# Conversion of the float64 weights written out slot by slot over block 0's FFN, in an attention and FFN kernel on one Trainium2 core

## The chip, the cores and the metric

The kernel runs on one core of a Trainium2 chip. The metric is device microseconds (us) from the start to the end of one execution; several executions are timed and the median counts. Lower is better. Engines are named as in the profile: PE (TensorE, matmul; PEld is its weight load), DVE (VectorE), ACT (ScalarE), POOL (GpSimd), SP (SyncE, which here issues most DMAs).

## The reference

Two stages. The first is an attention-like recurrence with a 48x48 state for each of 4 sequences and 8 heads, over 768 positions; the second a two-layer FFN on the 3072 rows of 384 values that the first one leaves.

```
k_n = k / (norm(k) + 1e-6)
for t in range(768):
    y[t]  = q[t] @ state
    v_old = state @ k_n[t]            # over the key axis
    state = state + beta[t] * outer(k_n[t], v[t] - v_old)
x = y as [3072, 384]
h = x @ w_in                          # [384, 2048]
out = max(0.01 * h, h) @ w_out        # [2048, 384]
```

The two weight matrices come as float64; the kernel computes in float32, and converts the weights on the chip, by bit operations on the raw 8-byte words.

## The kernel before

**Blocks.** The 768 positions are cut into 12 blocks of 64; one block of the 4 sequences is 256 token rows. The recurrence inside a block is replaced by a triangular system of 64 steps for each of the 32 sequence-head pairs. A block n needs, in this order: `gram(n)` (products of k with k and with q on PE, tiles pg, pq, and their masking by DVE into rq), `inv` (the norms in `norms`, then 31 elimination steps on DVE in `eliminate`, lines L390 and L395, on a tile T; blocks 0 and 1 are inverted together as T0, block 2 as T1, block 3 as T2 and so on), `solve(n)` (merging the inverted halves, tiles pz and pu; then pk, pw, py, pc on PE, each copied out of PSUM by ACT into rt, rv, ys), `columns(n)` (transposes px, and the split of x into xh on ACT, L123, and xl on DVE, L124) and `ffn(n)`. From block 2 on the inverse goes through DRAM: T to the DRAM tiles td and tt, and from these to the squares sq, which the matmuls pz and pu of `merge_z` and `merge_u` read (L490).

**FFN.** `ffn(n)` runs over 16 chunks f of the 2048 hidden columns: matmuls ph (L725), the leaky relu on ACT into gh (L728), and matmuls po (L715), which run two chunks behind. Block 0 uses plain float32 weights w32, views of the tiles cg: 3 matmuls of ph and 2 of po for each chunk. Every later block uses the format fp32r in two parts (high and low, tile w): 9 matmuls of ph and 6 of po for each chunk, a second relu on ACT, and gl by a subtraction on DVE (L733).

**Weights.** Eight pieces j of two chunks each. A raw piece wr is loaded by SP. Then, all in the generator `weights()`: the top 16 bits of each word are packed as bfloat16 into cg (on ACT, L155, for j of 0 to 3; on DVE, L158, for 4 to 7); four DVE operations with bits (L159, L162, L163, L165) build sign, exponent and first mantissa bits, the last of them into a tile ch of its own; ACT spreads ch over cg (L167); and `finish()` ors in the other mantissa bits on DVE (L176). After that cg holds the float32 piece, which block 0's FFN reads. `lows()` later makes the two parts for the blocks that follow: ACT rounds cg into the high part (L188), DVE subtracts for the low part (L190). There are NG = 4 buffers for cg, so `weights()` calls `lows()` for piece j-4 before it starts piece j; the parts w4 to w7 are made at the end of block 0 and at the start of block 1. The tile w of a piece takes the place of its raw words wr.

**What sets the order.** Each engine runs its instructions in program order. `weave` calls the generators in turn, slot by slot (a slot is about one chunk f of the FFN); the tuples SV, IV and GG give the slots between which `solve`, `inv` and `gram` of the next blocks are spread. Before block 0's FFN the calls are written out one by one. A scheduler then orders within those bounds; `behind(name)` keeps an instruction behind the last one recorded in `mark[name]` on its engine.

Of the kernel before, what the change touches and what calls it, by code (L numbers as in the profile page):

```python
# [26 lines left out]
NGR = NSEQ // GS  # L27
# [20 lines left out]
def delta_moe_kernel(ctx: ExitStack, tc, kq0, kqT, kv, qT, beta, cst, w_all, out, nblk):  # L48
# [89 lines left out]
    later, w32 = [], {}

    def weights():  # L140

        left = []
        for j in range(NJ):
            if j >= NG:
                next(lw)
            raw = raws.pop(j)
            mid = raw.bitcast(U32).rearrange("p (n two) -> p two n", two=2)[:, 0]
            top = raw.bitcast(BF16).rearrange("p (n four) -> p four n", four=4)[:, 2]  # L150
            g = sb.tile([P, 4 * DO], F32, tag=f"c{j % NG}", name=f"cg{j}", bufs=1)
            gi = g.bitcast(U32)
            a, x = gi[:, 0:2 * DO], gi[:, 2 * DO:]
            if j in BYA:
# [13 lines left out]
            left.append((j, g, mid))  # L168
            while left[1 if KA <= j < NJ - 1 or not j else 0:]:
                finish(*left.pop(0))  # L170
            yield

    def finish(j, g, mid):
        gi = g.bitcast(U32)
        with behind("work"):
            i = nc.vector.scalar_tensor_tensor(gi, mid, 13, gi, ALU.logical_shift_right, ALU.bitwise_or)  # L176
        mark["conv"] = mark["gl"] = i.ins
        later.append((j, g))
        for e in range(2):
            w32[2 * j + e] = g[:, e * 2 * DO:(e + 1) * 2 * DO]  # L180

    def lows():
        while True:
            j, g = later.pop(0)
            t = sb.tile([P, 8 * DO], F32R, tag=f"w{j}", name=f"w{j}", bufs=1)
            hi, lo = t[:, 0:4 * DO], t[:, 4 * DO:]
            with behind("xh"):
                nc.scalar.copy(hi, g)  # L188
            with behind("conv"):
                nc.vector.tensor_tensor(lo, g, hi.bitcast(F32), ALU.subtract)  # L190
            for y, part in enumerate((hi, lo)):
                for e in range(2):
                    for x, w in enumerate((wi, wo)):
                        w[y][2 * j + e] = part[:, (2 * e + x) * DO:(2 * e + x + 1) * DO]
            yield
# [10 lines left out]
    def first():  # L206
# [69 lines left out]

# [405 lines left out]
    def columns(n):  # L682

        need(sv, solve, n)
        xs[n] = parts = []
        px = [ps_a.tile([P, 2, TB], F32, tag="a", name=f"px{n}_{i}") for i in range(2)]
        part = [px[cc // 2][:, cc % 2] for cc in range(NCC)]
        for cc, x in enumerate(part):
            for g in range(NGR):
                i = nc.tensor.transpose(x[:, g * P:(g + 1) * P], ys[n, g][:, cc * P:(cc + 1) * P], eye)  # L690
        mark["px"] = i.ins
        for cc, x in enumerate(part):
            if not n:
                parts.append(sb.tile([P, TB], F32, tag="xh", name=f"x0_{cc}", bufs=3))
                if not cc % 2:
                    mark["xh"] = nc.scalar.copy(parts[-1], x).ins
                else:
                    mark["x"] = nc.vector.tensor_copy(parts[-1], x).ins
                continue
            xh, xl = (sb.tile([P, TB], F32R, tag=t, name=f"{t}{n}_{cc}", bufs=3) for t in ("xh", "xl"))  # L700
            split(x, xh, xl)
            parts.append((xh, xl))

    def ffn(n):
# [15 lines left out]
        for f in range(NFC):  # L720
            ph = hbank[f % 2][:, f // 2 % 2]
            ways = [(wi[y][f], x[cc][e], cc) for cc in range(NCC) for y, e in ((0, 0), (0, 1), (1, 0))] if n else [
                (w32[f], x[cc], cc) for cc in range(NCC)]
            for k, (w, a, cc) in enumerate(ways):
                i = nc.tensor.matmul(ph, w[:, cc * P:(cc + 1) * P], a, start=(k == 0), stop=(k + 1 == len(ways)))  # L725
            mark["ph"] = i.ins
            gh = sb.tile([P, TB], F32R if n else F32, tag="gh", name=f"gh{n}_{f}", bufs=FB)
            i = nc.scalar.activation(gh, ph, AF.Prelu, alpha=0.01)  # L728
            gl = None
            if n:  # L730
                gl = sb.tile([P, TB], F32R, tag="gl", name=f"gl{n}_{f}", bufs=FB)
# [36 lines left out]
    def weave(n_slots, *streams):

        taken = [0] * len(streams)  # L770
        for i in range(n_slots):
            for k, (gen, steps, a, b) in enumerate(streams):
                want = steps if i >= b - 1 else min(steps, max(0, i + 1 - a) * steps // (b - a))
                while taken[k] < want:
                    next(gen, None)
                    taken[k] += 1
# [107 lines left out]
```

## Time and profile before

| | before |
|---|---|
| median of 3 runs | 643.58 us (642.8 to 644.76) |
| the profiled execution | 642.36 us |
| its span, first to last instruction | 640.5 us |
| PE busy | 587.3 us, 92% of the span |
| DVE busy | 437.5 us, 68% |
| ACT busy | 324.0 us, 51% |
| mean granted TensorE clock | 0.979 |

All times inside an execution are counted from the span's start. The profiled execution lies 1.2 us under the median and takes 1.9 us more than its span. Busy shares are means over the whole span: the first 60 us, in which the first inverse and the first solve run, and the blocks 0 to 2 behind them look different from the blocks after them. A wait names the engine and line that ended it; an engine can also stand still because an instruction ahead of it in its own queue waits.

### The profile page before, as it was taken

To read this page: it belongs to the slowest core of one execution; us is meant where nothing else is said; L and a number is where in the kernel's file an instruction comes from. 1 tells how busy PE (TensorE), PEld (TensorE's weight loads), DVE (VectorE), ACT (ScalarE), POOL (GpSimd) and SP (SyncE) were. 2 spreads that over 40 slices of the span, in tenths; PEclk is the share of its full clock that TensorE was granted. 3 is DMA by queue.
4 is the path that set the end of the run, shared out by engine and by line. 5 is a ranking of instruction groups with operands and counts; after the bars stand their busy time and mean duration, and the time that the engine had idled before them with its cause. 6 is when DMAs were issued, how large, how long until landed. Compare 5 with 4: busy or idle time off the path is not lost.

```text
span 640.5 us, 22374 instructions
## 1 busy us (share of the span) xinstructions
PE 587.3 (92%) x9122; PEld 537.7 (84%) x9122; DVE 437.5 (68%) x1953; ACT 324.0 (51%) x812; POOL 10.7 (2%) x17
## 2 busy tenths in 40 slices
PE   5266987999889999999999999999999999999996
PEld 4245775799677988999999999999999999999996
DVE  3997796998936967859759759759759669331211
ACT  3466845464445544645645536545545545545322
POOL 6000000000000000000000000000000000000000
PEclk9986997999989999999999999999999999999999
DMA  6983754051257362254353352462461540410101
GB/s 122 316 241 125 248 154 111 12 124 27 36 101 157 79 130 55 61 97 104 72 97 95 76 114 71 90 126 47 96 139 27 104 105 4 79 30 3 26 2 26
DMA packets 123431, 59.69 MB, mean 93 GB/s; under 512 B 111296, under 2 KB 114496, under 8 KB 122304
## 3 DMA queue, kind: packets, MB, share of 16 engines
q1 hardware_dynamic: 120576, 57.27, 39.4%
q10 hardware_dynamic: 2752, 0.98, 0.8%
q8 instruction: 72, 1.18, 0.8%
q14 instruction: 31, 0.25, 0.1%
HBM read 46.96 MB, written 11.27 MB: 91 GB/s over the span
## 4 chain that ended last, share of the span: by engine, by line
PE 73%; ACT 3%; DMA 3%; SPq 2%; issue 2%; DVE 1%; ACTq 0%; DVEq 0%
PE ph L725 30%; PE po L715 28%; PE pk L620 3%; PE py L657 3%; PE pw L637 2%; PE pc L647 2%; PE pg L309 2%; DMA tt<-T 1%; PE px L690 1%; PE pu L490 1%; ACT w L188 1%; ACT gh L728 1%; PE pz L490 1%; DMA sq<-tt 1%; DMA td<-T 1%
## 5 line engine op out<-in xcount | busy, mean ns | idle before, releaser
L725 PE MATMUL ph<-xh,w 128*128 128x256 f32 x1056 | 224.5, 289 | 1.7 <-ACT xh L123 1.4
L725 PEld LDWEIGHTS ph<-xh,w 128*128 128x128 f32 x1056 | 174.9, 189 | 8.9 <-ACT xh L123 1.8
L733 DVE TENSOR_TENSOR gl<-ph,gh 128x256 fp32r<-128x256 f32 x176 | 74.3, 423 | 148.3 <-ACT ph L732 146.0
L715 PE MATMUL po<-w,gh 128*128 128x384 f32 x704 | 171.4, 342 | 4.1 <-ACT gh L728 4.1
L728 ACT ACTIVATE gh<-ph 128x256 fp32r<-128x256 f32 (+1 forms) x192 | 73.6, 384 | 170.3 <-PE ph L725 160.5
L725 PE MATMUL ph<-xl,w 128*128 128x256 f32 x528 | 149.3, 284 | 0.0
L715 PEld LDWEIGHTS po<-w,gh 128*128 128x128 f32 x704 | 121.4, 188 | 8.3 <-ACT gh L728 6.7
L395 DVE TENSOR_TENSOR T<-T,tmp 128x60 f32<-128x60 f32 (+35 forms) x661 | 112.3, 207 | 0.8
L390 DVE TENSOR_TENSOR tmp<-T,L 128x60 f32<-128x60 f32 (+35 forms) x661 | 112.2, 208 | 0.9
L715 PE MATMUL po<-w,gl 128*128 128x384 f32 x352 | 105.1, 338 | 0.0
L725 PEld LDWEIGHTS ph<-xl,w 128*128 128x128 f32 x528 | 100.1, 190 | 1.3 <-DVE xl L124 0.3
L732 ACT ACTIVATE ph<-ph 128x256 f32<-128x256 f32 x176 | 66.9, 380 | 0.0
L715 PEld LDWEIGHTS po<-w,gl 128*128 128x128 f32 x352 | 60.8, 188 | 0.4 <-issue 0.4
L622 ACT ACTIVATE rt<-pk 48x512 f32<-48x512 f32 x44 | 26.1, 594 | 25.1 <-PE pk L620 24.3
L326 DVE TENSOR_TENSOR rq<-pg,csb 64x256 f32<-64x256 f32 x80 | 33.9, 423 | 4.6 <-ACT gs L313 3.2
L725 PE MATMUL ph<-x,cg 128*128 128x256 f32 x96 | 26.6, 423 | 4.3 <-DVE rq L269 4.3
L639 ACT COPY rv<-pw 64x384 f32<-64x384 f32 x48 | 22.8, 474 | 10.2 <-PE pw L637 9.3
L657 PEld LDWEIGHTS py<-rv,rq 128*32 128x32 f32 x1536 | 19.3, 114 | 9.8 <-ACT rv L639 5.0
L725 PEld LDWEIGHTS ph<-x,cg 128*128 128x128 f32 x96 | 19.7, 211 | 9.1 <-ACT w L188 4.5
L649 ACT COPY rv<-pc 48x384 f32<-48x384 f32 x44 | 20.9, 475 | 12.3 <-PE pc L647 11.8
L657 PE MATMUL py<-rv,rq 128*32 128x48 f32 x1536 | 21.3, 213 | 6.1 <-ACT rv L639 4.8
L715 PE MATMUL po<-cg,gh 128*128 128x384 f32 x64 | 23.9, 499 | 0.0
(100 smaller groups left out, 587.5 us busy)
## 6 DMA issues: line engine op xcount, KB each, us to landing
wr<-in_w_all SPq DMA_DIRECT2D x8, 1536.0 KB, 11.4
kq<-in_kqT SPq DMA_DIRECT2D x40, 192.0 KB, 3.7
L<-gd SPq DMA_DIRECT2D x20, 256.0 KB, 4.0
rk<-in_kv SPq DMA_DIRECT2D x24, 192.0 KB, 3.5
rv<-in_kv SPq DMA_DIRECT2D x24, 192.0 KB, 3.9
rq<-in_qT SPq DMA_DIRECT2D x24, 192.0 KB, 3.7
out<-ob SPq DMA_DIRECT2D x46, 96.0 KB, 2.2
td<-T SPq DMA_DIRECT2D x40, 64.0 KB, 2.7
```

The lines of the kernel that those rows point to most:

```text
L326: nc.vector.tensor_tensor(qa[DN, c, b * NPAIR:(b + 1) * NPAIR], pv[b][r, 1], tri[r].rearrange("p (o t) -> p o t", o=1).broadcast_to([C, NP ...
L390: nc.vector.tensor_tensor(tv, t[:, :, j:j + 1].broadcast_to([P, k, w]), L[:, j, j + 1:].rearrange("p (o w) -> p o w", o=1).broadcast_to([P ...
L395: mark["steps"] = nc.vector.tensor_tensor(t, t, tv, ALU.subtract).ins
L622: nc.scalar.mul(t[UP, c], pv[c * 64:c * 64 + D].rearrange("p (y v) t -> p y v t", y=2), -1.0)
L639: d = nc.scalar.copy(v[DN, c], pv[c * 64:c * 64 + C])
L649: nc.scalar.copy(v1[UP, c], pv[c * 64:c * 64 + D])
L657: nc.tensor.matmul(pv[a:a + HC, u * D:(u + 1) * D], qa[:, c, u, e * HC:(e + 1) * HC], v[:, c, u], start=True, stop=True)
L715: i = nc.tensor.matmul(po[t][:, :DO], a[:, ts_], w, start=(f == 0 and k == 0), stop=(f == NFC - 1 and k + 1 == len(ways)))
L725: i = nc.tensor.matmul(ph, w[:, cc * P:(cc + 1) * P], a, start=(k == 0), stop=(k + 1 == len(ways)))
L728: i = nc.scalar.activation(gh, ph, AF.Prelu, alpha=0.01)
L732: i = nc.scalar.activation(ph, ph, AF.Prelu, alpha=0.01)
L733: mark["gl"] = nc.vector.tensor_tensor(gl, ph, gh.bitcast(F32), ALU.subtract).ins
```

## The change

The generators `weights()`, `finish()` and `lows()` become plain functions `pack`, `conv`, `expand`, `final` and `lows`, called for each piece at a place that is written out: for the first pieces between the calls ahead of block 0, and for the rest in a table `work` with a row for each slot of block 0 and three of block 1. All eight packs stand on ACT (L148). `conv` is the four operations on DVE (now L158 to L161), of which the last one writes into cg itself; the tile ch is gone. `expand` on ACT (L168) and `final` on DVE (L175) do piece 0 in two halves. There are five cg buffers. `lows` (ACT L184, DVE L186) stand in slots 4, 6, 8, 14 and 15 of block 0 and 1, 3 and 5 of block 1. Three packs instead of four stand ahead of the inverse; the masks rq of blocks 0 and 1 (now L264) stand ahead of `conv(0)` and `conv(1)`; a fifth raw piece is loaded early. T1's slots begin at 9 instead of 10, and the gram of block 2 at slot 2 instead of 5. The squares sq lie in the buffers c3 and c4.

```diff
-                next(lw)                      # in weights(), for j >= NG
...
-                nc.scalar.copy(x.bitcast(BF16), top)
...
-                    nc.vector.tensor_scalar(x.bitcast(BF16), top, -HI_MAX, HI_MAX, ALU.max, ALU.min)
...
-            h = sb.tile([P, 2 * DO], U32, tag="ch", name=f"ch{j}", bufs=2)
-            mark["work"] = nc.vector.scalar_tensor_tensor(h, x, 0xC000C000, a, ALU.bitwise_and, ALU.bitwise_or).ins
-            with behind("rv" if j == 1 else "xh"):
-                nc.scalar.copy(g, h.bitcast(BF16))
...
+    def pack(j, gate=None):
+        raw = raws.pop(j)
+        g = sb.tile([P, 4 * DO], F32, tag=f"c{j % NG}", name=f"cg{j}", bufs=1)
...
+        with behind(gate):
+            nc.scalar.copy(x.bitcast(BF16), top)
...
+    def conv(j):
...
+            after(nc.vector.scalar_tensor_tensor(x, x, 0xC000C000, a, ALU.bitwise_and, ALU.bitwise_or))
+    def expand(j, gate, e=slice(0, 2)):
...
+            nc.scalar.copy(g[:, a:b], g.bitcast(BF16)[:, 4 * DO + a:4 * DO + b])
+    def final(j, e=slice(0, 2)):
...
+            after(nc.vector.scalar_tensor_tensor(gi, mid[:, a:b], 13, gi, ALU.logical_shift_right, ALU.bitwise_or))
...
-                    with behind("x" if n else "work"):     # the masks rq of blocks 0 and 1
+                    with behind("dv" if n else "inverse"):
...
-            squares[x] = t = sb.tile([P, GU, P], F32, tag=f"c{x}", name=f"sq{x}", bufs=1)
+            squares[x] = t = sb.tile([P, GU, P], F32, tag=f"c{x + 3}", name=f"sq{x}", bufs=1)
...
+    for j in range(NPACK):
+        pack(j)
     weave(1, (iv, NI, 0, 1))
-    weave(1, (wg, 1, 0, 1))
     next(fg)
-    weave(1, (sv, NS, 0, 1))
-    weave(1, (wg, KA - 1, 0, 1))
+    conv(0)
+    weave(1, (sv, 4, 0, 1))
+    for j in (5, 6):
+        load_w(j, "dv")
     next(fg)
+    load_w(7, "dv")
+    conv(1)
+    lo, hi = slice(0, 1), slice(1, 2)
+    expand(0, "rv", lo)
+    final(0, lo)
+    weave(1, (sv, 2, 0, 1))
     next(gg)
+    expand(0, "xh", hi)
+    final(0, hi)
+    work = {
+        0: ((expand, 1, "xh"), (conv, 2)),
+        1: ((final, 1), (pack, 3, "h0_0"), (expand, 2, "h0_1")),
+        2: ((conv, 3), (final, 2), (pack, 4, "h0_1")),
+        3: ((expand, 3, "h0_3"),),
+        4: ((conv, 4), (final, 3), (lows, 0, "h0_4")),
+        5: ((expand, 4, "h0_5"), (pack, 5, "h0_4")),
+        6: ((conv, 5), (final, 4), (lows, 1, "h0_6")),
+        7: ((expand, 5, "h0_7"), (pack, 6, "h0_6")),
+        8: ((conv, 6), (final, 5), (lows, 2, "h0_8")),
+        9: ((expand, 6, "h0_9"), (pack, 7, "h0_8")),
+        10: ((conv, 7), (final, 6),),
+        11: ((expand, 7, "h0_11"),),
+        12: ((final, 7),),
+        14: ((lows, 3, "h0_14"),), 15: ((lows, 4, "h0_15"),),
+        NF + 1: ((lows, 5, "h1_1"),), NF + 3: ((lows, 6, "h1_3"),), NF + 5: ((lows, 7, "h1_5"),)}
...
-WAHEAD, WEARLY = 2, 4
-BYA = (0, 1, 2, 3)
-NG = 4
-KA, WB = 2, 12
-IV, GG = ((10, 17), (6, 17), (6, 17), (2, 17)), ((5, 7), (1, 2), (1, 2))
+WEARLY, NPACK, NG = 5, 3, 5
+KA = 2
+IV, GG = ((9, 17), (6, 17), (6, 17), (2, 17)), ((2, 4), (1, 2), (1, 2))
```

**DVE between the first inverse and the first FFN matmul.** Here rq are the masks (rq_78 and rq_79 of block 0, rq_80 and rq_81 of block 1), cg the pieces, x_1 a third of block 0's x. Before:

```order
L473 COPY rt_83<-tc 32x16x32
L159 TENSOR_SCALAR cg_679<-cg_679 128x768
L162 TENSOR_SCALAR cg_679<-cg_679 128x1536
L163 TENSOR_SCALAR cg_679<-cg_679 128x768
L165 SCALAR_TENSOR_TENSOR ch_684<-cg_679 128x768
L269 TENSOR_TENSOR rq_78<-pq_341,csb 64x2x256
...
L176 SCALAR_TENSOR_TENSOR cg_679<-wr_250,cg_679 128x1536
L131 MEMSET wr_957 128x1
L176 SCALAR_TENSOR_TENSOR cg_922<-wr_252,cg_922 128x1536
...
L698 COPY x_1_918<-px_0_908 128x256
L269 TENSOR_TENSOR rq_80<-pq_341,csb 64x2x256
```

And now:

```order
L467 COPY rt_83<-tc 32x16x32
L264 TENSOR_TENSOR rq_78<-pq_343,csb 64x2x256
...
L158 TENSOR_SCALAR cg_409<-cg_409 128x768
...
L264 TENSOR_TENSOR rq_80<-pq_343,csb 64x2x256
...
L264 TENSOR_TENSOR rq_81<-ph_73,csb 64x2x256
...
L161 SCALAR_TENSOR_TENSOR cg_411<-cg_411 128x768
L175 SCALAR_TENSOR_TENSOR cg_409<-wr_250,cg_409 128x768
L693 COPY x_1_941<-px_0_931 128x256
L175 SCALAR_TENSOR_TENSOR cg_409<-wr_250,cg_409 128x768
L158 TENSOR_SCALAR cg_413<-cg_413 128x768
```

The masks of both blocks stand ahead of the x copy, and of the full or-ins L176 of two pieces and a third piece's operations only half an or-in is left ahead of it.

**ACT in the second half of block 0.** rt, rv and ys are what `solve` copies out, gs what `gram` does. Before:

```order
L728 ACTIVATE gh_7_1278<-ph_73 128x256
L622 ACTIVATE rt_82<-pk_0_1159 48x2x256 x2
L622 ACTIVATE rt_83<-pk_1_1180 48x2x256 x2
L313 COPY gs_0_1203<-pg_0_0_1205 128x256
...
L728 ACTIVATE gh_8_1367<-ph_72 128x256
L167 CAST cg_1285<-ch_1290 128x1536
```

And now:

```order
L723 ACTIVATE gh_6_1257<-ph_72 128x256
L184 CAST w_1266<-cg_411 128x1536
L723 ACTIVATE gh_7_1272<-ph_73 128x256
L168 CAST cg_1210<-cg_1210 128x1536
L148 COPY cg_1277<-wr_845 128x1536
L616 ACTIVATE rt_82<-pk_0_1212 48x2x256 x2
L616 ACTIVATE rt_83<-pk_1_1233 48x2x256 x2
L723 ACTIVATE gh_8_1352<-ph_72 128x256
L184 CAST w_1361<-cg_413 128x1536
L723 ACTIVATE gh_9_1437<-ph_73 128x256
L168 CAST cg_1277<-cg_1277 128x1536
L148 COPY cg_1442<-wr_852 128x1536
```

A high part, a pack and an expansion of three different pieces now stand between the relus, and cg_1277, packed between gh_7 and gh_8, is expanded behind gh_9.

**Where block 2's inverse ends.** T_1506 and T_1482 are T1; gl_f stands for chunk f of block 1. DVE before:

```order
L733 TENSOR_TENSOR gl_10_2314<-ph_72,gh_10_2312 128x256
L395 TENSOR_TENSOR T_1506<-T_1506,tmp_29_0_1766 128x8x2
...
L395 TENSOR_TENSOR T_1506<-T_1506,tmp_30_0_1772 128x8
...
L733 TENSOR_TENSOR gl_11_2352<-ph_73,gh_11_2350 128x256
```

DVE now, with two of the low parts (L186):

```order
L186 TENSOR_TENSOR w_1933<-cg_1277,w_1933 128x1536
L384 TENSOR_TENSOR tmp_29_0_1762<-T_1482,L_1074 128x16
L728 TENSOR_TENSOR gl_4_1947<-ph_72,gh_4_1945 128x256
...
L389 TENSOR_TENSOR T_1482<-T_1482,tmp_30_0_1768 128x8
L728 TENSOR_TENSOR gl_5_2000<-ph_73,gh_5_1998 128x256
L186 TENSOR_TENSOR w_2009<-cg_1442,w_2009 128x1536
```

T1's last step stood between chunks 10 and 11 and stands between chunks 4 and 5. On PE its first reader pz stood here before:

```order
L715 MATMUL po_1_1788<-w_2097,gh_14_2578 128x384 x2
L490 MATMUL pz_1972<-sq_1960,gm_1204 32x128 x8
```

and stands here now:

```order
L710 MATMUL po_1_1784<-w_1685,gh_8_2159 128x384 x2
L484 MATMUL pz_1968<-sq_1956,gm_1077 32x128 x8
```

It moved from behind chunk 14's second layer to behind chunk 8's.

## Rows read from the trace of the kernel before

**Rows 1.** Source view of L124 (xl), one row per block start.

```profile
L124 DVE TENSOR_TENSOR xl<-px,xh x3: 415/424/425, 123.0 to 124.8; 128x256 fp32r<-128x256 f32 x3
...
L124 DVE TENSOR_TENSOR xl<-px,xh x3: 415/425/426, 180.9 to 182.8; 128x256 fp32r<-128x256 f32 x3
...
L124 DVE TENSOR_TENSOR xl<-px,xh x3: 415/415/425, 233.8 to 235.0; 128x256 fp32r<-128x256 f32 x3
...
L124 DVE TENSOR_TENSOR xl<-px,xh x3: 414/424/425, 326.9 to 328.2; 128x256 fp32r<-128x256 f32 x3
```

**Rows 2.** Windows: us, busy PE, PEld, DVE, ACT, POOL, clock, DMA share, GB/s.

```profile
41.40:154.30 112.90, 99.15 (x1428) 81.67 (x1429) 95.89 (x254) 65.67 (x122) 0.00 (x0) 0.89 0.41 117
60.00:123.00 63.00, 57.55 (x793) 43.85 (x794) 50.08 (x101) 33.24 (x60) 0.00 (x0) 0.92 0.44 133
...
98.00:104.00 6.00, 4.96 (x40) 3.23 (x42) 2.33 (x2) 2.77 (x6) 0.00 (x0) 0.50 0.27 76
```

**Rows 3.** Timeline of PE: start, us, line, out<-in, idle before and what ended it.

```profile
43.95 1.76 PE L507 MATMUL pz<-rt,gm 32*32 32x32 f32 x58 [6.21 <-ACT rt L473]
...
60.04 3.33 PE L725 MATMUL ph<-x,cg 128*128 128x256 f32 x7 [4.26 <-DVE rq L269]
```

**Rows 4.** Timeline of DVE, 40 to 61 us.

```profile
40.65 0.75 DVE L473 COPY rt<-tc 32x512 f32<-32x512 f32 x2
41.44 0.56 DVE L159 TENSOR_SCALAR cg<-cg 128x768 uint32<-128x768 uint32 x1
...
43.23 0.96 DVE L165 SCALAR_TENSOR_TENSOR ch<-cg 128x768 uint32<-128x768 uint32 x1
44.22 1.28 DVE L269 TENSOR_TENSOR rq<-pq,csb 64x512 f32<-64x512 f32 x2
...
54.22 1.76 DVE L176 SCALAR_TENSOR_TENSOR cg<-wr,cg 128x1536 uint32<-128x1536 uint32 x1 [3.07 <-ACT cg L167]
...
57.56 0.42 DVE L698 COPY x<-px 128x256 f32<-128x256 f32 x1
...
59.21 1.30 DVE L269 TENSOR_TENSOR rq<-ph,csb 64x512 f32<-64x512 f32 x2
```

**Rows 5.** Timeline of ACT, 38 to 45 us.

```profile
41.65 1.61 ACT L155 COPY cg<-wr 128x1536 bf16<-128x1536 bf16 x1 [3.85 <-DMA wr<-in_w_all]
43.28 1.14 ACT L473 COPY rt<-tc 32x512 f32<-32x512 f32 x2
```

**Rows 6.** Waits, 60 to 123 us: total, times, longest.

```profile
DVE cg L158 <- PE po L715: 9.2, 2, 6.0
...
PEld ph L725 <- ACT w L188: 4.5, 1, 4.5
```

**Rows 7.** Groups by form, DVE 40:135 and ACT 20:135: busy us, mean ns, idle before.

```profile
L158 DVE TENSOR_SCALAR cg<-wr 128x1536 bf16<-128x1536 bf16 x4 | 3.8, 961 | 9.4 <-PE po L715 9.2
...
L155 ACT COPY cg<-wr 128x1536 bf16<-128x1536 bf16 x4 | 6.4, 1589 | 12.9 <-DMA wr<-in_w_all 12.8
...
L167 ACT CAST cg<-ch 128x1536 f32<-128x1536 bf16 x8 | 11.7, 1472 | 5.2 <-DVE ch L165 5.1
L188 ACT CAST w<-cg 128x1536 fp32r<-128x1536 f32 x8 | 11.4, 1485 | 0.0
```

**Rows 8.** Chain that ended last, 120 to 200 us: start, us, what.

```profile
124.46 5.30 ACT w L188 x4
...
138.59 1.07 PE ph L725 x9
139.67 1.05 PE po L715 x6
...
156.11 3.97 DMA td<-T
```

**Rows 9.** Timeline of DVE at T1's last step; tile view of sq.

```profile
154.10 0.17 DVE L395 TENSOR_TENSOR T<-T,tmp 128x8 f32<-128x8 f32 x1
...
L490 PE MATMUL pz<-sq,gm x32: 269/273/297, 165.3 to 193.6; 128*32 128x128 f32 x32
```

More of the change, by code (lines that the diff above doesn't have):

```diff
@@ L136, in signs @@
         nc.scalar.mul(neg, eye, -1.0)
[L138 to L146, printed above, removed]
-                next(lw)
[L148 to L154, printed above, removed]
-                nc.scalar.copy(x.bitcast(BF16), top)
-            with behind("x" if j == KA else "conv" if j > KA else "work" if j else "inverse"):
-                if j not in BYA:
-                    nc.vector.tensor_scalar(x.bitcast(BF16), top, -HI_MAX, HI_MAX, ALU.max, ALU.min)
-                i = nc.vector.tensor_scalar(a, x, 0x7FFF7FFF, None, ALU.bitwise_and)
-            if j + WAHEAD >= WEARLY:
-                load_w(j + WAHEAD, "work")
+    parts, w32 = {}, {}
@@ new lines, in pack, with after @@
+    def pack(j, gate=None):
+        raw = raws.pop(j)
+        g = sb.tile([P, 4 * DO], F32, tag=f"c{j % NG}", name=f"cg{j}", bufs=1)
+        x = g.bitcast(U32)[:, 2 * DO:]
+        top = raw.bitcast(BF16).rearrange("p (n four) -> p four n", four=4)[:, 2]
+        parts[j] = g, raw.bitcast(U32).rearrange("p (n two) -> p two n", two=2)[:, 0]
+        with behind(gate):
+            nc.scalar.copy(x.bitcast(BF16), top)
+    def after(inst):
+        mark["gl"] = mark["dv"] = inst.ins
+    def conv(j):
+        gi = parts[j][0].bitcast(U32)
+        a, x = gi[:, 0:2 * DO], gi[:, 2 * DO:]
+        with behind("dv"):
+            nc.vector.tensor_scalar(a, x, 0x7FFF7FFF, None, ALU.bitwise_and)
@@ L168, in weights @@
[L168 to L179, printed above, removed]
-            w32[2 * j + e] = g[:, e * 2 * DO:(e + 1) * 2 * DO]
@@ L182, in lows @@
[L182 to L195, printed above, removed]
+            after(nc.vector.scalar_tensor_tensor(x, x, 0xC000C000, a, ALU.bitwise_and, ALU.bitwise_or))
@@ new lines, in expand @@
+    def expand(j, gate, e=slice(0, 2)):
+        g = parts[j][0]
+        a, b = e.start * 2 * DO, e.stop * 2 * DO
+        with behind(gate):
+            nc.scalar.copy(g[:, a:b], g.bitcast(BF16)[:, 4 * DO + a:4 * DO + b])
+    def final(j, e=slice(0, 2)):
+        g, mid = parts[j]
+        a, b = e.start * 2 * DO, e.stop * 2 * DO
+        gi = g[:, a:b].bitcast(U32)
+        with behind("dv"):
+            after(nc.vector.scalar_tensor_tensor(gi, mid[:, a:b], 13, gi, ALU.logical_shift_right, ALU.bitwise_or))
+        for e in range(e.start, e.stop):
+            w32[2 * j + e] = g[:, e * 2 * DO:(e + 1) * 2 * DO]
@@ new lines, in lows @@
+    def lows(j, gate):
+        g = parts[j][0]
+        t = sb.tile([P, 8 * DO], F32R, tag=f"w{j}", name=f"w{j}", bufs=1)
+        hi, lo = t[:, 0:4 * DO], t[:, 4 * DO:]
+        with behind(gate):
+            nc.scalar.copy(hi, g)
+        with behind("dv"):
+            after(nc.vector.tensor_tensor(lo, g, hi.bitcast(F32), ALU.subtract))
+        for y, part in enumerate((hi, lo)):
+            for e in range(2):
+                for x, w in enumerate((wi, wo)):
+                    w[y][2 * j + e] = part[:, (2 * e + x) * DO:(2 * e + x + 1) * DO]
@@ L271, in first @@
                           tri[r].rearrange("p (o v t) -> p o v t", o=1, v=1).broadcast_to([C, 2, NPAIR, C]), ALU.mult)
-            if not n:
-                mark["mask"] = d.ins
+            after(d)
             done.add((gram, n))
@@ L697, in columns @@
                 else:
-                    mark["x"] = nc.vector.tensor_copy(parts[-1], x).ins
+                    with behind("dv"):
+                        after(nc.vector.tensor_copy(parts[-1], x))
                 continue
@@ L766, in chain, with weave_at, weave @@
             yield from fn(n)
[L768 to L776, printed above, removed]
+    taken = {}
+    def weave_at(i, n, *streams):
+        for gen, steps, a, b in streams:
+            key = gen, n, a
+            want = steps if i >= b - 1 else min(steps, max(0, i + 1 - a) * steps // (b - a))
+            while taken.get(key, 0) < want:
+                next(gen, None)
+                taken[key] = taken.get(key, 0) + 1
+    def weave(n, *streams):
+        for gen, steps, a, b in streams:
+            for i in range(steps):
+                next(gen, None)
     NS, NF, NI = NSLOT, NFC + 1, HC + 1
-    wg, lw = weights(), lows()
     fg, gg = first(), chain(gram, range(2, nblk))
@@ L815 @@
-LL, AG = 2, 6
+KA = 2
+IV, GG = ((9, 17), (6, 17), (6, 17), (2, 17)), ((2, 4), (1, 2), (1, 2))
 SV = (0, 10), (3, 13), (1, 11), (2, 12)
```

12 lines of the change are left out of this document (8 added, 4 removed).

## The prediction

> **What bounds the kernel now.** I read block by block first. The first xl of a block marks its start [rows 1]: blocks 1 and 2 take 57.9 us (123.0 to 180.9) and 52.9 us (to 233.8), the two behind them 46.55 us each ((326.9 - 233.8) / 2). So there are some 60 us ahead of block 0's FFN, 63 us of block 0, and then 11.35 and 6.35 us by which blocks 1 and 2 exceed the rest. The change acts on these stretches alone.
>
> The timelines tell what holds each. The first FFN matmul waits for DVE's masks and starts at 60.04 [rows 3]; DVE reaches those masks last, behind two or-ins and part of a third piece [rows 4]. In block 0 PE is busy for 57.55 of 63 us [rows 2], and DVE stands still for 9.2 us in two waits until block 0's matmuls po have let a cg buffer go [rows 6]. At the block boundary four high parts in a row, 5.30 us, lie on the chain that ended last, and PE's weight loads wait 4.5 us for one of them [rows 8, 6]. T1's last step ends at 154.3, and the first pz that needs it runs at 165.3, 11.0 us later, by way of DRAM [rows 9, 8]. DVE is at work for 95.89 of the 112.9 us up to there [rows 2]: block 2's inverse is late since DVE is full, with 17.0 us idle.
>
> **Part 1, the start.** DVE's rows give the new time of the first matmul. The rt copies end at 41.4. The four masks of a block take two groups of two, 1.28 and 1.30 us, so 2.58; a conversion runs from 41.44 to 44.22, 2.78 us with its gaps; half an or-in is half of 1.76, 0.88; the x copy is 0.42 [rows 4]. In the new order: 41.44 + 2.58 + 2.78 + 2.58 + 2.78 + 0.88 + 0.42 + 0.1 for two small memsets = **53.6**. PE has to be ready for that: before, ACT did a pack at 41.65 ahead of the rt copies that pz waited for (6.21 us) [rows 5, 3]; without it and one full expansion (1.47 [rows 7]) between them the solve ends about 3 us sooner, 52 to 53, so DVE stays the later one. Gain 60.04 - 53.6 = 6.4; ends 4.5 (DVE waits for half an expansion, 0.7, and the solve is 1.2 late) and 7.5 (all gaps gone).
>
> **Part 2, block 0.** Taken from DVE: four packs of 0.961, 3.84 us. Given to ACT: four of 1.589, 6.36 us [rows 7]. Here the packs are weighed against a rule. By these rows a pack costs ACT 1.65 times what it costs DVE, 2.5 us more engine time in all, and I let it pass since ACT was busy for only 33.24 of the 63 us [rows 2]. The Trainium skill, in "ScalarE: Activation LUTs", section "Rules for kernel authors", says to put max and min on VectorE and not on ScalarE, which by its figure would be up to about three times slower per element in bf16. By that figure the four packs would cost ACT 4 x 0.961 x 3 = 11.5 us, an estimate from that page, 5.2 more than the rows give; the row's ratio has the same sign and is smaller, and the sum uses the row.
>
> ACT's load in block 0 also grows by three high parts (before, two of its five stood ahead of 60 us; 3 x 1.485 = 4.5) and one further early pack (1.6): 33.24 + 6.36 + 4.5 + 1.6 is about 46 of some 57 us. ACT is no longer idle cover, but not full. What goes from PE's side: its idle 63.0 - 57.55 = 5.45, and the stretch 98 to 104, where the clock was 0.50 (1.2 GHz) and 4.96 us of matmuls [rows 2] would have taken about half, 2.5. Together 7.9. What comes: on ACT pack 6 waits for the low part of piece 1, about 1.7 us (one or-in or subtraction of 1.76 [rows 4] behind it on DVE), and behind it stand relus and expansions; on DVE the conversion of piece 6 waits for its pack, 1.6 [rows 7]. I take **5.5** gained, ends 2 and 8. Block 0's last ph then ends 11.9 us sooner than before.
>
> **Part 3, block 2's inverse.** To T1's last step DVE does less: four packs (3.84), five gl that stood ahead of it and now stand behind it (one subtraction of 256 columns is like the x copy, 0.42, or xl, 0.42 [rows 4, 1]: 2.1), one low part (1.76) and the scaling of v for block 2's solve, which follows pz (four, priced as four instructions like xl but with one and a half times the columns, about 2.0). In all 9.7, so 95.89 - 9.7 = 86.2 busy. Of its 17.0 idle the 9.2 behind po and 3.07 behind an expansion [rows 6, 4] go, 4.7 stays, and the waits of part 2 add 3.3: 41.4 + 86.2 + 4.7 + 3.3 = 135.6, so **136** in place of 154.3, 18 sooner. Ends: 127.6 (no idle left) and 144.6 (all 17.0 come back).
>
> But that doesn't reach the end. The way through DRAM still takes 11.0 us [rows 9], so pz can run at 147; and pz has moved forward by six chunks on PE. PE reaches it at about 143: T1's last step stands just ahead of chunk 5's gl, and chunk 8's second layer is some three chunks of 2.13 (1.07 + 1.06, [rows 8]) after that. PE thus stands for 4 to 5 us. From pz to block 2 it was 180.9 - 165.3 = 15.6; now six more chunks follow, 12.8, which fill about 0.8 of the solve's gaps: 147 + 15.6 + 12.8 - 0.8 = **174.6**; ends 172.5 and 177.8. Against 180.9 that is a gain of 6.3. Of the 11.9 at the end of block 0 about half is given back in this wait. The 5.30 us of high parts at the boundary [rows 8] are cost-free in this sum, since DVE's T1 is later than what they held; if T1 is early they count (below).
>
> **Part 4, after that.** T2's slots are as before, so its way through DRAM stands in the same place in block 2, whose excess of 6.35 stays. From block 3 on nothing is changed. The three late low parts in block 1 take 3 x 1.485 on ACT and 3 x 1.76 on DVE that were at the boundary before; they are in the sum of part 3. Larger buffers and the moved squares cost at most one memset like the others, nothing to 1 us.
>
> **Sum.** The profiled execution took 642.36; less 6.4 is 636.0. It lies 1.22 under the median of the runs, so against 643.58 the forecast is **637.0**. No change that a measurement can tell is within 0.3%, 1.9 us.
>
> **Rivals.** *Bigger gain.* If DVE ends T1 near 128, pz finds its squares there (128 + 11 = 139 against PE at its place), and the 11.9 of block 0's end reaches block 2 whole, with some of block 1's 11.35 excess on top, the 5.30 at the boundary first. 12 to 18 us, 625 to 631 against the median. For it: 9.2 of DVE's 17.0 idle are one kind of wait, and five buffers take that one away. Against it: gl and steps share DVE, so a later step holds PE too. Chance 0.23.
>
> *No change.* The 6.4 of the start is eaten before block 2: T1 at 144.6 puts pz at 155.6 and block 2 at 183, as late as before within 2. Or the moved pieces stall just as long at their new places, since the order is fixed but the waits are not. 641.7 to 645.5. Chance 0.11.
>
> *Slower: ACT's queue.* Packs 5, 6 and 7 each need a buffer whose old piece has had its low part taken by DVE, and a raw piece that comes late; behind each in ACT's queue stand the relus that PE's second layer waits for. One round is a high part, a pack and an expansion, 1.485 + 1.589 + 1.472 = 4.55 [rows 7], three times 13.6. PE stood at 0.50 where it had waited (98 to 104, six us with 4.96 of matmuls [rows 2]); after three more such stops it loses about 1.6 each, 4.7. Together 18.3, less the 11.9 of the start and block 0: 6.4 slower, **650**. It decides if ACT's waits in front of packs sum to over 12 us. For it: ACT's 46 of 57 us leaves little to catch up in. The rule of the Trainium skill in part 2 ("ScalarE: Activation LUTs", "Rules for kernel authors") points this way too. Against it: the packs stand one slot behind the low part they need, 57 / 16 = 3.5 us. Chance 0.16.
>
> **How the numbers follow.** The forecast's own case, 632 to 641.6, has 0.50; bigger gain 0.23; no change 0.11; slower 0.16. Faster by over 0.3%: 0.73; same 0.11; slower 0.16. The range reaches from the lower edge of the bigger gain to just past no change, 624 to 646, which leaves out most of the slower case and the tail of the bigger gain, 0.2.
>
> **What would show it.** Part 1: the first ph at 53 to 54, waiting for a DVE copy or or-in rather than for a mask. Part 2: the wait of DVE for po gone, block 0's last ph near 110, and ACT's busy time in block 0 near 46; wrong if ACT waits before packs for over 5 us in all. Part 3: T1's last step at 134 to 138, a wait of PE at pz of 3 to 6 us in block 1, and the first xl of block 2 at 172 to 178; if PE doesn't wait at pz, the bigger gain is right. Part 4: block 2 again 52 to 54 us long, and 46.5 after it.

## The result, and the profile after

| | before | after |
|---|---|---|
| median | 644.0 us (642.21 to 646.92, 6 runs) | 637.16 us (634.95 to 640.81, 6 runs) |
| the profiled execution | 642.36 us | 637.35 us |
| its span | 640.5 us | 635.6 us |
| PE / DVE / ACT busy | 587.3 / 437.5 / 324.0 us | 585.4 / 433.3 / 329.5 us |
| mean granted clock | 0.979 | 0.978 |

The ratio is 0.9895, with a 95% interval of 0.9857 to 0.9933. The forecast of 637.0 is met almost to the digit. The way to it is not, as the starts of the blocks show. The source view of L124 in the profile after, rows as [rows 1]:

```profile
L124 DVE TENSOR_TENSOR xl<-px,xh x3: 418/420/427, 119.8 to 122.8; 128x256 fp32r<-128x256 f32 x3
...
L124 DVE TENSOR_TENSOR xl<-px,xh x3: 414/424/424, 172.9 to 174.1; 128x256 fp32r<-128x256 f32 x3
...
L124 DVE TENSOR_TENSOR xl<-px,xh x3: 415/415/424, 230.0 to 231.2; 128x256 fp32r<-128x256 f32 x3
...
L124 DVE TENSOR_TENSOR xl<-px,xh x3: 414/424/425, 322.1 to 323.3; 128x256 fp32r<-128x256 f32 x3
```

Block 2 starts 8.0 us sooner than before, block 3 only 3.8, and block 5 4.8: block 2 itself has become longer, 57.1 us in place of 52.9. The timeline of PE and that of DVE, with windows of the profile after (columns as in [rows 2]):

```profile
40.21 1.38 PE L501 MATMUL pz<-rt,gm 32*32 32x32 f32 x58 [1.87 <-ACT rt L467]
...
44.16 1.65 PE L631 MATMUL pw<-rv,rt 128*32 128x48 f32 x67
49.30 1.41 PE L631 MATMUL pw<-rv,rt 128*32 128x48 f32 x58 [3.49 <-issue]
50.44 0.30 PE L651 MATMUL py<-rv,rq 128*32 128x48 f32 x3
50.52 0.28 PE L631 MATMUL pw<-rv,rt 128*32 128x48 f32 x1
50.52 1.57 PE L651 MATMUL py<-rv,rq 128*32 128x48 f32 x65
55.61 1.49 PE L651 MATMUL py<-rv,rq 128*32 128x48 f32 x60 [3.51 <-issue]
...
59.07 1.22 PE L720 MATMUL ph<-x,cg 128*128 128x256 f32 x2 [0.25 <-ACT x L690]
...
147.91 0.65 PE L484 MATMUL pz<-sq,gm 128*32 128x128 f32 x16 [1.04 <-DMA sq<-tt]
```

```profile
138.36 0.17 DVE L389 TENSOR_TENSOR T<-T,tmp 128x8 f32<-128x8 f32 x1
```

```profile
46.00:49.30 3.30, 0.00 (x0) 0.00 (x0) 3.22 (x7) 0.74 (x2) 0.00 (x0) 0.50 0.89 223
52.10:55.60 3.50, 0.00 (x0) 0.00 (x0) 0.96 (x1) 1.09 (x2) 0.00 (x0) 0.50 1.02 426
98.00:104.00 6.00, 6.00 (x145) 4.55 (x137) 5.65 (x14) 5.24 (x8) 0.00 (x0) 1.00 0.01 3
```

Four things stand there. The solve does begin 3.7 us sooner than in [rows 3], but PE then stops twice for 3.5 us, in the middle of a row of like matmuls, for "issue", that is for nothing that the profile shows; the first FFN matmul comes at 59.07, not at 53.6. In block 0 the stretch 98 to 104, which ran at 0.50 before [rows 2], is at full clock and full. T1's last step is at 138.36, and PE waits for the squares of pz for 1.04 us.

### The profile page after: what moved, and what is told of

It reads as the page before. It is cut to its first block, busy times and chain, and to the rows that moved or that the text cites. A ratio compares the mean times of both kernels' runs of the same rounds, so it can differ in the third digit from the quotient of the medians.

```text
span 635.6 us, 22372 instructions
## 1 busy us (share of the span) xinstructions
PE 585.4 (92%) x9122; PEld 536.6 (84%) x9122; DVE 433.3 (68%) x1949; ACT 329.5 (52%) x817; POOL 10.7 (2%) x17
## 4 chain that ended last, share of the span: by engine, by line
PE 72%; DVE 17%; ACT 4%; issue 4%; DMA 2%; SPq 1%; DVEq 0%; ACTq 0%
PE ph L720 28%; PE po L710 27%; DVE tmp L384 4%; DVE T L389 4%; PE pk L614 3%; PE pw L631 3%; PE py L651 2%; PE pc L641 2%; PE pg L303 2%; DVE rq L320 2%; DVE cg L175 2%; DVE w L186 1%; PE px L684 1%; ACT gh L723 1%; PE pz L484 1%
## 5 line engine op out<-in xcount | busy, mean ns | idle before, releaser
L710 PE MATMUL po<-w,gh 128*128 128x384 f32 x704 | 173.2, 344 | 4.9 <-ACT gh L723 4.9
L720 PE MATMUL ph<-x,cg 128*128 128x256 f32 x96 | 25.2, 407 | 0.2 <-ACT x L690 0.2
L631 PEld LDWEIGHTS pw<-rv,rt 128*32 128x32 f32 x1536 | 19.1, 114 | 7.0 <-issue 4.4
L631 PE MATMUL pw<-rv,rt 128*32 128x48 f32 x1536 | 21.4, 213 | 3.5 <-issue 3.5
```

Source lines behind the costliest of these rows:

```text
L631: nc.tensor.matmul(pv[a:a + HC, u], t[:, c, u // NPAIR, u % NPAIR, e * HC:(e + 1) * HC], v[:, c, u], start=True, stop=True)
L710: i = nc.tensor.matmul(po[t][:, :DO], a[:, ts_], w, start=(f == 0 and k == 0), stop=(f == NFC - 1 and k + 1 == len(ways)))
```

## The experiments

Every kernel is compared with runs of the kernel before on its own chip; those medians were 644.1 (e1 to e4), 643.59 (e5 to e8) and 643.83 (e9 to e12).

**Are the two stops waits for instructions behind weight loads?** Two edits move loads of raw pieces out of the first solve; a third makes the kernel before load one more piece early.

```diff
 e1_late_loads, to the changed kernel; e2_late_loads_4 has it too
-    for j in (5, 6):
-        load_w(j, "dv")
     next(fg)
-    load_w(7, "dv")
...
-        0: ((expand, 1, "xh"), (conv, 2)),
+        0: ((load_w, 5, "dv"), (expand, 1, "xh"), (conv, 2)),
 and load_w for 6 in slot 2, for 7 in slot 4
 e2_late_loads_4, in addition
     conv(1)
+    load_w(4, "dv")
-WEARLY, NPACK, NG = 5, 3, 5
+WEARLY, NPACK, NG = 4, 3, 5
 e4_before_5_early, to the kernel before
-WAHEAD, WEARLY = 2, 4
+WAHEAD, WEARLY = 2, 5
```

> The changed kernel with the loads of the raw pieces 5, 6 and 7 moved out of the first solve into slots 0, 2 and 4 of block 0; the early load of piece 4 stays. Theory A (in the changed kernel PE's two stops of 3.5 us in the first solve, ended by 'issue', are waits for its own instructions, which come late while the DMA engines are full with raw weights): the second stop (52.1 to 55.6) goes, the first one (46 to 49.3), which begins before pieces 5 and 6 are issued, may stay; first FFN matmul near 55.5 in place of 59.07, time 3 us less, about 634. Theory B (the stops have another cause, such as a copy on ACT or the clock at 1.2 GHz): both stay, time 637.

> As the run before, and piece 4 too is loaded only after the second conversion. Theory A: both stops go, first FFN matmul at 53.5 to 54.5, which is what DVE's sum gave, and T1's last step some 4 us sooner; time 4 to 5 us less than the changed kernel, 632 to 633. Theory B: both stops stay, 637. Theory C (the start is gained, but block 2's inverse or the blocks behind it eat it): first FFN matmul at 54, but time 636 to 638.

> The kernel before, with five raw pieces loaded early in place of four (one number). Theory A: PE stops for about 3.5 us once in the first solve, for 'issue', between 44 and 50 us, though no line of the solve has changed; since the first FFN matmul waits 4.3 us for DVE's masks there, the time stays within 1.5 us of the kernel before. Theory B: no such stop.

Measured: e1 636.19 us (ratio 0.9885, 0.9852 to 0.9918), e2 **632.01** (0.9837, 0.9802 to 0.9872; 630.69 to 634.9 over 6 runs, all below the lowest of the changed kernel's, 634.95), e4 641.72 in one run. PE's timeline in e1, e2 and e4, in this order:

```profile
50.24 1.41 PE L631 MATMUL pw<-rv,rt 128*32 128x48 f32 x58 [3.81 <-issue]
...
53.80 0.90 PE L651 MATMUL py<-rv,rq 128*32 128x48 f32 x60 [0.77 <-ACT cg L168]
```

```profile
44.11 3.08 PE L631 MATMUL pw<-rv,rt 128*32 128x48 f32 x125
...
49.62 0.87 PE L651 MATMUL py<-rv,rq 128*32 128x48 f32 x60 [1.21 <-ACT cg L168]
...
52.99 2.83 PE L720 MATMUL ph<-x,cg 128*128 128x256 f32 x12 [1.24 <-DVE cg L175]
```

```profile
48.78 1.41 PE L637 MATMUL pw<-rv,rt 128*32 128x48 f32 x58 [0.64 <-issue]
...
52.07 0.87 PE L657 MATMUL py<-rv,rq 128*32 128x48 f32 x60 [0.57 <-issue]
```

Theory A holds for the long stops of the changed kernel: without pieces 5 and 6 the second one goes and the first one stays; without piece 4 the first one goes too in e2's profiled execution, and the first FFN matmul is at 52.99 and waits for half an or-in on DVE, as the prediction's sum had it (53.6). B falls, and C too: e2's time fell by 5. The 3 us expected of e1 did not come; its time can't be told from the changed kernel's. Something is left of the stops: at the same row of py PE still stands for 0.77 us in e1 and 1.21 us in e2. The profile puts that down to ACT's expansion of cg, which py does not read (more at the end). In e4 the size of A fails: stops appear at the same two instructions, but of 0.64 and 0.57 us; its DMA load is over when PE gets there (share 0.55 in 46 to 49.3, 0.04 in 49.3 to 52.1). So an early piece alone costs little there; of e4's time one run tells nothing. The kernels with e2's loads that follow below (e7, e11, e12) have a first stop of 1.63, 0.55 and 1.29 us: late loads make the stops short, but do not always end them.

**Does the move of packs to ACT matter?**

```diff
 e3_pack_on_dve, to the changed kernel, in pack()
+        if j < 4:
+            with behind(gate):
+                nc.scalar.copy(x.bitcast(BF16), top)
+        else:
+            with behind("dv"):
+                after(nc.vector.tensor_scalar(x.bitcast(BF16), top, -HI_MAX, HI_MAX, ALU.max, ALU.min))
```

> The changed kernel with packs 4 to 7 back on DVE (0.96 us each), at the same places. If DVE's sum sets block 2's inverse, as the prediction has it: DVE gets 3.84 us more ahead of T1's last step (138.6), so that and block 2's start come 2 to 4 us later, time 639 to 641. If ACT's queue is what holds block 0 (the slower rival): ACT is relieved of 6.4 us, relus come sooner, time 634 to 636.

638.29 us (0.9921, 0.9888 to 0.9953): its interval overlaps the changed kernel's, so the time tells nothing. In its profile T1's last step is at 140.31, 1.95 later, and block 2 starts at 174.0, 1.1 later. The sign is DVE's, the size below the expected range, and the slower rival is not seen: ACT relieved of 6.4 us made nothing sooner.

**Which part of the order matters?** Two number pairs in the changed kernel are put back together (e5), that of the inverse is put back alone (e9), and that of the gram is moved alone in the kernel before (e10).

```diff
 e5_old_slots, to the changed kernel
-IV, GG = ((9, 17), (6, 17), (6, 17), (2, 17)), ((2, 4), (1, 2), (1, 2))
+IV, GG = ((10, 17), (6, 17), (6, 17), (2, 17)), ((5, 7), (1, 2), (1, 2))
 e9_old_inverse_slot, to the changed kernel
+IV, GG = ((10, 17), (6, 17), (6, 17), (2, 17)), ((2, 4), (1, 2), (1, 2))
 e10_before_gram_early, to the kernel before
-IV, GG = ((10, 17), (6, 17), (6, 17), (2, 17)), ((5, 7), (1, 2), (1, 2))
+IV, GG = ((10, 17), (6, 17), (6, 17), (2, 17)), ((2, 4), (1, 2), (1, 2))
```

> The changed kernel with the old slots for block 2's inverse (10 to 17) and its gram (5 to 7). If DVE's sum alone sets T1's end, as the prediction has it, the slots do not matter: T1's last step within 1.5 us of 138.6, time 636.5 to 638.5. If the order sets it: T1 later by a slot or more, 3 to 6 us, block 2's start 2 to 5 us later, time 639 to 642.

> The changed kernel with the old slots for block 2's inverse (10 to 17) alone; its gram stays at 2 to 4. The run with both old slots gave 643.44; there ACT's packs wait 5.9 us for DVE's low parts, which stand behind the gram's masks, and PE waits 5.9 us for ACT's rv. Theory G (it is the gram's place that counts): no such wait, 636 to 639. Theory I (the inverse's slots count): 641 to 644.

> The kernel before with block 2's gram at slots 2 to 4 in place of 5 to 7, nothing else of the change. There too ACT stood 5.12 us in front of an expansion whose words DVE made only behind the eight masks of the gram, and PE waited 4.8 us for rv behind it, with the clock at 0.50 afterwards. Theory G: that wait of PE goes, block 0 is 4 to 7 us shorter, time 638 to 641. Rival (only together with five buffers and the new order of the weights): the wait moves to another place, time 642.5 to 645.

e5 took 643.44 us (ratio 1.0, 0.9982 to 1.0018): **the whole gain is gone**. T1's last step is at 145.83 there and block 2's start at 181.27, 7.5 and 8.4 later than in the changed kernel, which is past both expectations. e9 took 638.04 (0.9907, 0.9878 to 0.9937), no different from the changed kernel. And e10, the kernel before with nothing but its gram moved from slots 5 to 7 to slots 2 to 4, took **636.18** (0.9878, 0.9844 to 0.9912), lower than the 638 to 641 expected: as fast as the whole change. What the gram's place does is seen in timelines. ACT and PE before:

```profile
97.02 1.47 ACT L167 CAST cg<-ch 128x1536 f32<-128x1536 bf16 x1 [5.12 <-DVE ch L165]
```

```profile
99.04 0.37 PE L657 MATMUL py<-rv,rq 128*32 128x48 f32 x4 [4.82 <-ACT rv L639]
```

DVE, ACT and PE in e5:

```profile
94.54 1.75 DVE L320 TENSOR_TENSOR rq<-pg,csb 64x256 f32<-64x256 f32 x4
...
96.91 1.75 DVE L320 TENSOR_TENSOR rq<-pg,csb 64x256 f32<-64x256 f32 x4
...
99.31 1.76 DVE L186 TENSOR_TENSOR w<-cg,w 128x1536 fp32r<-128x1536 f32 x1
```

```profile
101.10 1.54 ACT L148 COPY cg<-wr 128x1536 bf16<-128x1536 bf16 x1 [4.72 <-DVE w L186]
```

```profile
103.18 0.38 PE L651 MATMUL py<-rv,rq 128*32 128x48 f32 x4 [5.91 <-ACT rv L633]
```

With the gram at slots 5 to 7 its eight masks and their copies, 4.7 us on DVE, stand ahead of what ACT's next instruction waits for (before, among the operations whose words an expansion needs; in e5, ahead of the low part that a pack needs); behind that one in ACT's queue stands rv, and PE waits 4.8 or 5.9 us for it and falls to half clock (0.50 from 98 to 104 before [rows 2], and from 104 to 108 in e5). This is the mechanism of the prediction's slower rival, packs in ACT's queue that wait for DVE's low parts; it was in the kernel before in another dress, and with the earlier gram PE's wait for rv is gone in both kernels. In e10's window and in PE's wait there:

```profile
98.00:104.00 6.00, 4.20 (x19) 2.45 (x17) 5.84 (x6) 3.74 (x6) 0.00 (x0) 1.00 0.02 7
```

```profile
100.66 1.53 PE L725 MATMUL ph<-x,cg 128*128 128x256 f32 x6 [1.80 <-DVE cg L176]
```

the clock is 1.00, and py waits for nothing. Other waits are left: PE stands 1.80 us for an or-in in that window, and ACT's expansions wait 9.4 us for DVE's words in block 0, where they waited 5.1 us before. But block 0 takes 58.5 us from the start of the first ph to that of the last (60.55 to 119.1), against 63.1 before (60.04 to 123.1).

**Are the five buffers worth anything by themselves?**

```diff
 e8_before_5_buffers, to the kernel before
-            h = sb.tile([P, 2 * DO], U32, tag="ch", name=f"ch{j}", bufs=2)
+            h = x
-NG = 4
+NG = 5
```

> The kernel before with five cg buffers in place of four and words expanded in place (which makes the room for the fifth); nothing else of the change. Theory (the buffers' wait of 9.2 us on DVE was a main part of what made block 2's inverse late): the wait of DVE for po goes, T1's last step comes 4 to 9 us sooner than 154.1, block 2's start 2 to 4 us sooner, time 640 to 642. Rival (the wait only moves to other instructions of the same piece): T1 within 2 us of 154, time 643 to 645.

645.37 us (1.0037, 1.0017 to 1.0057). The rows of PE, of DVE and of ACT in e8:

```profile
102.14 0.37 PE L657 MATMUL py<-rv,rq 128*32 128x48 f32 x4 [5.41 <-ACT rv L639]
...
154.30 0.64 PE L490 MATMUL pz<-sq,gm 128*32 128x128 f32 x16 [1.54 <-DMA sq<-tt]
```

```profile
134.60 0.17 DVE L395 TENSOR_TENSOR T<-T,tmp 128x8 f32<-128x8 f32 x1
```

```profile
127.89 6.99 ACT L188 CAST w<-cg 128x1536 fp32r<-128x1536 f32 x5
```

Half of the theory holds: DVE's wait for po is gone and T1 ends 19.5 us sooner than before, sooner even than in the changed kernel. But PE's wait for rv stays, 5.41 us where it was 4.82, block 2 starts at 182.4, 1.5 later than before, and the time is 0.4% longer. T1's end alone does not set block 2's start: pz waits for its squares until 154.30, 19.7 us after T1's last step. e8 does not weigh the buffers quite alone, since it has five high parts in a row at the boundary, 6.99 us, where the kernel before has four [rows 8].

e9 shows what T1's slots are worth. T1 ends at 146.59 there, 8.2 later than in the changed kernel, and pz is reached at 157.01 with no wait at all. Block 2 starts 3.7 later (176.65), but it takes 52.3 us in place of 57.1, so that block 3 starts 1.0 sooner (228.94). What the earlier slots gain in block 1 is lost in block 2.

**Is the block boundary free?**

```diff
 e6_lows_at_boundary, to the changed kernel
-        NF + 1: ((lows, 5, "h1_1"),), NF + 3: ((lows, 6, "h1_3"),), NF + 5: ((lows, 7, "h1_5"),)}
+        NF: ((lows, 5, "xh"), (lows, 6, "xh"), (lows, 7, "xh"))}
```

> The changed kernel with the parts of pieces 5, 6 and 7 made at the start of block 1, three in a row on ACT behind the split of x, as the kernel before did with four. The prediction called the 5.30 us at the boundary cost-free while T1 is later than what they held: block 1's first relus 3 to 4.5 us later, block 2's start unchanged, time 636 to 638.5. Rival: what the boundary holds up reaches block 2 whole, time 640 to 642.

640.25 us (0.9939, 0.9915 to 0.9964). ACT's timeline in e6:

```profile
123.28 4.23 ACT L184 CAST w<-cg 128x1536 fp32r<-128x1536 f32 x3
...
129.10 0.41 ACT L723 ACTIVATE gh<-ph 128x256 fp32r<-128x256 f32 x1
```

The first relu of block 1 is at 129.10, 4.9 later than the changed kernel's 124.16, and block 2 starts at 176.7, 3.8 later. The rival was right in the main: 3.8 of the 4.9 us that the boundary holds up reach block 2.

**Why is block 2 longer, and can it be had back?** ACT and PE at the end of block 2 in the changed kernel:

```profile
228.08 1.05 ACT L449 COPY T<-T 128x512 f32<-128x512 f32 x1 [5.13 <-DVE T L389]
228.94 0.40 ACT L723 ACTIVATE gh<-ph 128x256 fp32r<-128x256 f32 x1
```

```diff
 e7_late_loads_t3_early, to e2_late_loads_4
-IV, GG = ((9, 17), (6, 17), (6, 17), (2, 17)), ((2, 4), (1, 2), (1, 2))
+IV, GG = ((9, 17), (6, 17), (5, 16), (2, 17)), ((2, 4), (1, 2), (1, 2))
 e11_lows_slot_earlier, to e7
-        14: ((lows, 3, "h0_14"),), 15: ((lows, 4, "h0_15"),),
+        13: ((lows, 3, "h0_13"),), 14: ((lows, 4, "h0_14"),),
 e12_t2_slot_earlier, to e11
+IV, GG = ((9, 17), (5, 16), (5, 16), (2, 17)), ((2, 4), (1, 2), (1, 2))
```

> The kernel with the late loads of four pieces (632.0), and the inverse made in block 2 given the slots 5 to 16 in place of 6 to 17. In that kernel as in the changed one ACT's copy of this inverse stands right ahead of the last relu of block 2 and waits 5.1 us for DVE's last elimination steps; PE waits 2.2 us for the relu, and block 2 takes 55.2 us where the kernel before took 52.9. Theory (this order is what made block 2 longer): the wait of PE for that relu goes, block 2 takes 53 us or less, time 629.5 to 630.5. Rival (the steps just hold other relus and gl up in their new place, since DVE is full there): block 2 as long, time 631.5 to 633.

> The kernel of 628.87 (late loads, block 2's own inverse one slot earlier) with the low parts of pieces 3 and 4 a slot earlier, 13 and 14. There one of them stood on DVE between the first and the second xl of block 1, and PE waited 1.1 us for the second. Expected: that wait goes and block 1's first relu comes 1 to 2.5 us sooner; time 627 to 628.5. Rival: T1's steps are pushed back by as much, pz waits, and the time stays at 628.5 to 629.5.

> As the run before, and the inverse made in block 1 (that of block 3) starts a slot earlier, 5 to 16. In the kernel of 628.87 the first pz of block 3 waits 1.6 us for its squares. Expected: that wait goes, time 626 to 627.5. Rival: DVE is full there and gl come later, time 628 to 630.

e7 took **628.87 us** (0.9778, 0.9757 to 0.98; 4 runs from 628.67 to 628.95), a little below the 629.5 to 630.5 expected, the lowest median of all and faster than both kernels. Block 2 takes 51.9 us there (167.6 to 219.5) against 55.2 in e2 (168.0 to 223.2); block 3 is longer, 47.8 us (to 267.3) against 45.9 (to 269.1), so that 2.1 us are left at the start of block 5 (313.5 against 315.6). In the waits of the two, e2 first, the copy of the inverse and PE's wait behind it:

```profile
ACT T L449 <- DVE T L389: 5.1, 1, 5.1
...
PE po L710 <- ACT gh L723: 2.2, 1, 2.2
```

```profile
ACT T L449 <- DVE T L389: 2.5, 1, 2.5
...
PE po L710 <- ACT gh L723: 0.3, 1, 0.3
```

So in this order the copy of the inverse, placed by the scheduler right ahead of block 2's last relu, is one cause of the longer block. It is not the whole of it: e5 has the same two waits, of 5.3 and 2.2 us, in a block 2 of 53.0 us. e11 took 630.42 (0.9784, 0.9747 to 0.9821) and e12 630.03 (0.9787, 0.975 to 0.9824): neither can be told from e7. In e11 the wait for xl is gone and block 1's first relu comes 1.1 us sooner, but pz still waits 0.96 us for its squares and block 2 starts at 168.1. Its time lies above both expectations, and T1's steps were not pushed back, as the rival had it (133.87, against 134.13 in e7). In e12 the wait of block 3's pz is 1.5 as before, for another reason (ACT's gs), and nothing is gained.

## Why the prediction was right, and where it was not

Measured in the profiled executions, sooner than before:

| | predicted | measured |
|---|---|---|
| first FFN matmul | 6.4 | 1.0 (59.07) |
| first to last ph of block 0 | 5.5 | 5.7 |
| T1's last step | 18 | 15.7 (138.36) |
| first pz of block 2 | 18.3 | 17.4 (147.91) |
| block 2's start | 6.3 | 8.0 (172.9) |
| block 3's start | 6.3 | 3.8 (230.0) |
| the end of the span | 6.4 | 4.9 (635.6) |

**Part 1** failed at "so DVE stays the later one". DVE was there in time, but PE was not: 7.0 us of stops, for which the trace of before had no row, since there the DMA engines were nearly idle while that solve ran. The part is right for e2, where the long stops are gone. The loads were part of the change, and the step costed their issue but not what they would meet.

**Part 2** had the size, and the right rows: PE's idle time of 5.45 us and the half clock in 98 to 104 [rows 2]. The windows of the changed kernel from the first ph of block 0 to the last, and from the end of the first inverse to T1's last step:

```profile
59.10:116.40 57.30, 55.24 (x793) 42.32 (x794) 52.24 (x133) 45.00 (x70) 0.00 (x0) 0.95 0.35 92
...
41.40:138.50 97.10, 85.38 (x1297) 68.03 (x1293) 85.14 (x235) 66.19 (x113) 0.00 (x0) 0.88 0.46 126
```

In the first, PE's idle time fell to 2.1 us, and its busy time by 2.3, where the clock was given 2.5; ACT is busy for 45.0 us, with 46 forecast. The 5.5 does not follow from the part's own terms, though: 7.9 less waits of 1.7 and 1.6 is 4.6. And the part has no term for what made PE idle. What it weighs are the packs, and the buffers [rows 6] stand in part 3 and in the first rival; e8 and e3 show that neither does it, and e5, e9 and e10 that the gram's place does, which the prediction did not cost at all. With the old place the result would have been the rival "no change", by the mechanism of the slower one. The rule of the Trainium skill that was weighed there ("ScalarE: Activation LUTs", "Rules for kernel authors") is not what decided: by e3 the choice of engine for the four packs moves the time by less than the runs can tell.

**Part 3** had T1 and pz within 2.4 and 0.9 us. DVE's busy time from 41.4 to T1's last step is 85.1 us, with 86.2 forecast (six gl, and not five, moved behind T1); its idle time is 12.0 and not 8.0, of which 5.3 is one wait at the x copy, behind PE's stops. But "block 2's inverse is late since DVE is full" is not the reason that matters: T1's end as such decides little (e8, e9). PE was held for 1.0 us at pz, not 4 to 5: it got there at 146.9, not at 143, and the way through DRAM took 9.6 us (138.36 to 147.91), not 11.0. That block 0's end came 5.2 us later than forecast does not explain the short wait: in e2 the last ph starts at 112.2, 4.2 sooner than in the changed kernel (116.4), T1's last step comes sooner by as much (134.01), and PE is held for 0.97 us at pz there too. "The 5.30 us of high parts at the boundary [rows 8] are cost-free" is wrong: block 1's first relu came at 131.54 before and comes at 124.16 now, and e6 shows 3.8 us at block 2's start for three of the four casts.

**Part 4** failed at "whose excess of 6.35 stays". The slots are the same, but the scheduler put the next inverse's last steps and ACT's copy of it elsewhere within them, and block 2 grew by 4.2 us. e7 gets 3.3 back, and gives 1.9 of it up in block 3; e9, with T1's old slots, has a block 2 of 52.3 us.

So the errors of the start (5.4 too much) and of block 2 (4.2 too much) were made up by the wait at pz and the boundary, that were taken too high, and by 1.0 us in blocks 3 and 4; and the medians lie 6.8 apart where the two profiled executions lie 5.0 apart. The case that was given the highest chance came in, with a sum of which two terms fell; that the total is met to 0.2 us is luck.

What stays open: what the rest of the change is worth on top of the earlier gram. e2 and e7 stand against e10 with 632.01 and 628.87 against 636.18, and e10 has no long stop in the first solve either, but no run takes the parts of that difference apart. Open too is what part of e10's gain is clock and what is the wait itself.

## What to carry to other kernels

Where a queue's head waits, look at what stands in front of the work that it waits for, on the other engine, and not only at the two instructions named: here one pair of slot numbers for a stage that the weights have nothing to do with was worth the whole change. When an edit moves bulk loads, look at which stretch they will run in and at how densely an engine issues small instructions there (here 254 in 2.8 us). And a total that comes out right proves no term of its sum: the starts of the blocks tell which terms hold.

## What the runs showed of the hardware

PE stopped at the same two instructions in every kernel that stopped, with 58 matmuls of pw and 60 of py left; between them lie 127 matmuls and as many weight loads. In the changed kernel both stops are ended by "issue" and last 3.5 us, with a DMA share of 0.89 and 1.02. The Trainium skill, in "Runtime: NRT & Kernel Launch", section "Instruction fetch mechanics", says that an engine's instructions come in blocks of 256 over a DMA queue of the sequencer's own, and that the cost at a block's edge is mostly hidden. The 254 instructions between the stops agree with the blocks; 7.0 us of stops in 10 us do not agree with "mostly hidden". The page of the kernel before has a DMA queue of kind "instruction":

```profile
q8 instruction: 72, 1.18, 0.8%
```

That is 72 packets of 16 KB, for PE's 9122 matmuls and 9122 weight loads, 253 to a packet. In the trace of the changed kernel two of these packets ran from 46.45 to 47.84 and from 53.18 to 54.19, and PE went on at 49.30 and 55.61, 1.4 to 1.5 us behind each. The stops of e1 and e4 end 1.4 to 1.5 us behind such a packet too; so does the wait of 0.77 us of e1, and that of 1.21 us in e2 ends 1.6 us behind one, so these were probably of the same kind. The second packet began 3.9 us after PE had gone on in the changed kernel, with the DMA share at 1.00 from 49.3 to 52.1; it began 1.1 us after in e1 and 1.0 us after in e4, with a share of 0.26 and 0.04. The packet itself took about 1 us in all three. So the long stops come with a block that starts late while weights are loading; that it stands behind them in a queue is argued and not shown.

PE's clock was 0.50 (1.2 GHz) in both stops, but it had been so before them, from 41 us on; in e2 it was at 1.00 in the window 52.1 to 55.6:

```profile
52.10:55.60 3.50, 2.61 (x12) 2.11 (x12) 3.40 (x7) 3.37 (x5) 0.00 (x0) 1.00 0.77 267
```
